# Stores of two sequences split and put off around the first FFT stages of an FFT-mix-FFN kernel

## Chip, cores and metric

The kernel runs on one core of a Trainium2 chip. The metric is the device time of one execution in microseconds (us); lower is better.

## What is computed

The input `x` is 8 sequences of 3008 rows of 256 float32 values. The first part goes through a Fourier transform along the sequence, a complex mixing of the 256 channels with a bias, a soft threshold, and the inverse transform; the second part is a gated FFN over all 24064 rows.

```python
X = np.fft.rfft(x, axis=1)                      # 8 x 1505 x 256, complex
Yr = Xr @ w_r - Xi @ w_i + b_r
Yi = Xr @ w_i + Xi @ w_r + b_i
Yr = np.sign(Yr) * np.maximum(np.abs(Yr) - 0.01, 0.0)      # and Yi likewise
y = np.fft.irfft(Yr + 1j * Yi, n=3008, axis=1).astype(np.float32)
...
gate = 1.0 / (1.0 + np.exp(-(y @ w_gate)))      # 256 -> 1536
out = gate * (y @ w_val) @ w_out                # 1536 -> 256
```

## The kernel before

The transform of length 3008 is split as 47 x 64. A sequence passes through four stages, and between them its data goes through DRAM, since each stage wants it in another layout:

- **Stage A, 47 points** (`load_a`, `fwd_a`, `store_a`). A sequence's 8 blocks `h` of 384 KB are loaded to `xf` tiles; four matmuls with the table `fa_sb` transform each (two for the first half, two for the second); ScalarE and VectorE copy the result back over the same `xf` tile; the tile is stored to the DRAM tile `zd[b]`, 96 rows of it, two for each of the 48 values of `q`.
- **Stage B, 64 points** (`load_b`, `fwd_b`, line 237). A step works on two values of `q`, one from each of two groups; there are NP = 12 steps and two more that drain the pipeline. `load_b(b, q)` loads `zf`, 256 KB, rows `4q` to `4q + 3` of `zd[b]`: what one step reads was written by all 8 stores of stage A. `mf_sb` is the step's table.
- **Mix and inverse of stage B** (`mix4` for the first sequence, line 293; `inv_b`, line 305). The mix of step `q - 1` and the inverse of step `q - 2` (table `mi_sb`) run beside the forward of step `q`; the result `vz` goes to the DRAM tile `vd[b]`.
- **Inverse of stage A** (`load_v`, `inv_a`, line 340). A unit `u` loads `vf`, 192 KB, and makes 188 columns of `y`, split into a high and a low part by ScalarE and VectorE (`split_y`).

The FFN (`ffn1`, lines 399 to 401, and `ffn2`) works on chunks of 512 columns and 12 slices `f` of the hidden dimension. The first chunk needs the units 0, 1 and 2. Its weights come as 64-bit floats (`raw`), and are converted beside the first sequence's steps and the first chunk (`load_part`, `start_part`, `ops`).

The first sequence is done alone, then the second sequence's transform, and later ones, run beside the FFN. The order of this beginning is written out by hand in the `with tc.manual_schedule()` blocks: stage A of sequence 0, then the first four blocks (`EARLY`) of stage A of sequence 1, then the steps `q` of stage B with the remaining four blocks after the last of them, then the three inverse units and the first chunk of the FFN. Nearly all transfers are issued by SyncE, in the order of the code. GpSimd issues those of `vd` in the first sequence, the last four stores of sequence 1, and those of later sequences' half blocks (`azh`, line 199).

At three places TensorE is given matmuls whose result nobody reads (`keep_warm`): WARM = 13 at the start, WARM_Z = 10 between stage A and the first step, and WARM_V = 5 between the first and the second inverse unit (line 836).

The DRAM tile is what a load waits for: a `zf` load waits for the 8 stores to `zd[0]`, and a `vf` load for the 12 stores to `vd[0]`.

Of the kernel before, what the change touches and what calls it, by code (L numbers as in the profile page):

```python
# [9 lines left out]
F32 = mybir.dt.float32  # L10
# [9 lines left out]
R2, R1 = 47, 64  # L20
NK2 = 24
NQ = 2 * NK2
# [5 lines left out]
FFT_BANKS, L1_BANKS, L2_BANKS = 3, 3, 2  # L28
# [4 lines left out]

LAST_GAP, SIDE_GAP = 20, 3
PRE = 2
WARM = 13
WARM_Z, WARM_V = 10, 5
EARLY = 4
AT_FIRST = 3
NCONV = 7  # L40
# [69 lines left out]
def tile_fft_mix_ffn(ctx: ExitStack, tc, x, w_r, w_i, b_r, b_i, w_one, w_out, mf, mi, mis, fa, fb, out):  # L110
# [39 lines left out]
    fa_sb = cw.tile([2 * R2, 2 * NQ], F32, name="fa_sb")  # L150
    nc.scalar.dma_start(fa_sb, fa)

    zd = [tc.dram_tile([NQ, R1, D], F32, name=f"zd{b}") for b in range(B)]
    vd = [tc.dram_tile([NQ, R1, D], F32, name=f"vd{b}") for b in range(B)]
    td = tc.dram_tile([NH, 2, P, 8 * P], F32, name="td")
    md = tc.dram_tile([NK2, P, 2, P], F32, name="md")
    yd = tc.dram_tile([CT, P, B * S - T0], F32, name="yd").rearrange("t p n -> p t n")
    xv = x.rearrange("b u p (h c) -> b u p h c", c=D)
    zv = [z.rearrange("q (j h) c -> (q j) h c", j=2) for z in zd]
    vv = [v.rearrange("q (j h) c -> (q j) h c", j=2) for v in vd]  # L160

    held = {}
# [22 lines left out]

    def store_a(b, h, queue=nc.sync):
        queue.dma_start(zv[b][:, 4 * h:4 * h + 4], held.pop(("x", b, h))[:2 * NQ])

    def load_half(b, h):
        xf = r2k("xfh").bitcast(F32)  # L190
# [35 lines left out]

    def load_b(b, q):
        zf = p2.tile([P, 2, D], F32, tag="ld", bufs=NLD, name="zf")
        nc.sync.dma_start(zf, zd[b][4 * q:4 * q + 4].rearrange("(q a) n c -> (a n) q c", q=2))
        held["z", b, q] = zf  # L230

    def fwd_b(b, q, m, full):
# [251 lines left out]
    def ffn_units():  # L484
        units, todo = [], {}
        seq = [(c, f) for c in range(NPL) for f in range(NF)]

        def own(c):

            return range(-(-c * CW // UT), -(-(c + 1) * CW // UT))  # L490

        for c in range(1, NPL):
            at = (c - 1) * NF
            for i, u in enumerate(own(c)):
                todo.setdefault(at + (0, 3, 6)[i], []).append(lambda u=u: load_v(u))
                todo.setdefault(at + (3, 6, 9)[i], []).append(lambda u=u: inv_a(u))
            todo.setdefault(at + 1, []).append(lambda c=c: carry(c))

        def unit(n):
            c, f = seq[n]  # L500
            if n == 0:
                for i, u in enumerate(own(0)):
                    if i == 1:
                        w = w1h[:, 0].rearrange("p i t n -> p (i t n)")
                        keep_warm(bank("warm", "l1", L1_BANKS), w[:, :P], w, WARM_V)
                    inv_a(u)
            ffn1(c, f)
            for t in todo.pop(n, ()):
                t()
            if n >= LAG and n - LAG < len(seq) - BEHIND:  # L510
                ffn2(*seq[n - LAG])
        return [lambda n=n: unit(n) for n in range(len(seq))], own(0), own(NPL - 1)[-1] + 1
# [346 lines left out]
    with tc.manual_schedule():  # L859
# [2 lines left out]
        load_a(1, 0)  # L862
        for h in range(na):
            fwd_a(0, h)
            store_a(0, h)
            if h in (1, 3, 4):
                load_a(1, {1: 1, 3: 2, 4: 3}[h])
            if h == 2:
                load_mix()
# [4 lines left out]
        load_bias4()  # L874
        load_part()
        mfs[2] = load_mf(2)
        for h in range(EARLY):
            fwd_a(1, h)
            if h == 1:
                wi_sb = mix_weights()  # L880
        keep_warm(bank("warm"), zero[:, :P], zero, WARM_Z)
        for q in range(NP + 2):
            if q + 2 < NP:
                load_b(0, q + 2)
            if 0 <= q - 1 < NP:
                mis_[q - 1] = load_mi(q - 1, True)
            if q < 2:
                for h in range(q * EARLY // 2, (q + 1) * EARLY // 2):
                    store_a(1, h)
            if q == 3:  # L890
                nc.sync.dma_start(fb_sb, fb)
# [33 lines left out]
        for h in range(EARLY + 1, na):  # L925
            ops(left.pop(0), 0)
            fwd_a(1, h)
            store_a(1, h, nc.gpsimd)
        ops(left.pop(0), 0)
    p0s.close()  # L930
    p3 = p3s.enter_context(tc.tile_pool(name="p3", bufs=2, side="right", reuse_waits="tile"))
    with tc.manual_schedule():
        for u in own0:
            load_v(u)
        load_part()
        halves(AT_FIRST)
# [157 lines left out]
```

## Time and profile before

| | us |
|---|---|
| median of 3 runs | 2819.46 (2818.62 to 2820.18) |
| profiled execution | 2820.81 |
| its span, first to last instruction | 2819.0 |
| TensorE busy in it | 2802.4 |
| VectorE busy | 2082.3 |
| ScalarE busy | 1309.6 |
| GpSimd busy | 710.5 |

The span is that of one execution taken by the hardware profiler; the profiled execution's own time is 1.8 us longer, with what lies around the span. PE is TensorE, DVE VectorE, ACT ScalarE, POOL GpSimd, SP SyncE; a `q` behind an engine's name is its queue of issued transfers. L12 is line 12 of the kernel. The granted clock is a share of TensorE's full clock: 1.00 is 2.4 GHz, 0.50 is 1.2 GHz.

### The profile page before, as it was taken

The numbers are of one execution on the slowest core, as the hardware profiler recorded it, in microseconds if no ns is written. First come the engines' busy times: TensorE is split into PE (matmuls) and PEld (weight loads), VectorE is DVE, ScalarE is ACT, GpSimd is POOL, SyncE is SP. The second block draws the span as 40 slices with busy tenths as digits, with TensorE's granted clock in tenths as the row PEclk, the third lists the DMA queues.
The fourth block names the chain that finished last, engine by engine and source line by source line (L and its number), as shares of the span: only waits on it lengthen the run. The fifth ranks groups of instructions, "written<-read, shape, count | busy, mean of one in ns | idle before, by whom it ended". The sixth has DMA issues, their size and how long they took to land.

```text
span 2819.0 us, 38251 instructions
## 1 busy us (share of the span) xinstructions
PE 2802.4 (99%) x13896; PEld 2308.1 (82%) x13896; DVE 2082.3 (74%) x3109; ACT 1309.6 (46%) x2276; POOL 710.5 (25%) x638
## 2 busy tenths in 40 slices
PE   9999999999999999999999999999999999999999
PEld 6678888888899888888888888888888888888887
DVE  5777778667787536777777777777777777777776
ACT  4664544545455444444444444444444444444443
POOL 0211010224100002333333333333333343333321
PEclk9999999999999999999999999999999999999999
DMA  9866544666554661000000000000000000000000
GB/s 296 257 213 194 170 143 149 199 184 192 165 152 140 186 187 38 30 15 16 30 31 27 4 31 31 31 16 15 31 30 16 15 30 31 30 1 30 30 16 15
DMA packets 173469, 241.01 MB, mean 85 GB/s; under 512 B 14592, under 2 KB 124896, under 8 KB 173280
## 3 DMA queue, kind: packets, MB, share of 16 engines
q1 hardware_dynamic: 163776, 214.93, 24.8%
q0 software_dynamic: 9408, 23.60, 2.5%
q8 instruction: 110, 1.80, 0.3%
q14 instruction: 79, 0.65, 0.1%
q10 hardware_dynamic: 96, 0.04, 0.0%
HBM read 134.17 MB, written 104.33 MB: 85 GB/s over the span
## 4 chain that ended last, share of the span: by engine, by line
PE 94%; DVE 2%; DMA 2%; ACT 1%; issue 0%; SPq 0%; DVEq 0%; ACTq 0%
PE pd L659 11%; PE pa L659 11%; PE pc L659 11%; PE po L636 8%; PE po L635 8%; PE po L634 8%; PE pm L271 6%; PE pb L659 5%; PE pia L340 4%; PE pb L237 3%; PE pa L176 2%; PE pg L399 2%; PE pg L401 2%; PE pg L400 2%; PE pv L399 2%; PE pv L400 2%
## 5 line engine op out<-in xcount | busy, mean ns | idle before, releaser
L636 PE MATMUL po<-hl,w 128*128 128x512 f32 x912 | 362.5, 397 | 0.0
L635 PE MATMUL po<-hh,w 128*128 128x512 f32 x912 | 361.5, 396 | 0.0
L634 PE MATMUL po<-hh,w 128*128 128x512 f32 x912 | 360.8, 396 | 0.0
L718 POOL TENSOR_TENSOR c<-c,c 128x512 f32<-128x512 f32 x114 | 147.7, 1296 | 831.0 <-DVE c L714 640.1
L659 PE MATMUL pa<-a,w1h 128*128 128x512 f32 x912 | 284.0, 393 | 0.0
L659 PE MATMUL pc<-s,w1h 128*128 128x512 f32 x912 | 283.7, 392 | 0.0
L714 DVE TENSOR_TENSOR c<-u,pc 128x512 f32<-128x512 f32 x228 | 156.7, 687 | 114.7 <-PE pc L659 106.2
L689 DVE TENSOR_TENSOR u<-u,pb 128x512 f32<-128x512 f32 x228 | 155.3, 681 | 88.8 <-PE pb L659 62.6
L606 ACT CAST hh<-v 128x512 fp32r<-128x512 f32 x114 | 70.7, 620 | 306.2 <-DVE v L699 306.2
L636 PEld LDWEIGHTS po<-hl,w 128*128 128x128 f32 x912 | 171.5, 188 | 41.9
L634 PEld LDWEIGHTS po<-hh,w 128*128 128x128 f32 x912 | 172.0, 189 | 40.9
L635 PEld LDWEIGHTS po<-hh,w 128*128 128x128 f32 x912 | 171.0, 188 | 40.8
L659 PEld LDWEIGHTS pa<-a,w1h 128*128 128x128 f32 x912 | 171.2, 188 | 40.1
L659 PEld LDWEIGHTS pc<-s,w1h 128*128 128x128 f32 x912 | 171.0, 188 | 37.6
L610 POOL TENSOR_TENSOR hl<-c,hh 128x512 fp32r<-128x512 f32 x114 | 152.4, 1337 | 186.1 <-ACT hh L606 186.1
L271 PE MATMUL pm<-w_sb,xsh 128*128 128x256 f32 x1008 | 189.4, 288 | 1.4 <-ACT xf L177 1.1
L659 PE MATMUL pc<-s,w1l 128*128 128x512 f32 x456 | 177.5, 389 | 0.0
L659 PE MATMUL pa<-a,w1l 128*128 128x512 f32 x456 | 177.0, 388 | 0.0
L720 DVE TENSOR_TENSOR u<-u,pd 128x512 f32<-128x512 f32 x228 | 156.9, 688 | 24.5 <-DVE c L714 0.9
L693 DVE TENSOR_TENSOR v<-v,pc 128x512 f32<-128x512 f32 x228 | 156.6, 687 | 24.4 <-DVE v L691 0.5
L691 DVE TENSOR_TENSOR v<-u,pd 128x512 f32<-128x512 f32 x228 | 156.9, 688 | 24.0 <-DVE u L689 0.5
L685 ACT COPY u<-pa 128x512 f32<-128x512 f32 x228 | 133.7, 586 | 78.7 <-PE pa L659 78.6
(174 smaller groups left out, 6738.7 us busy)
## 6 DMA issues: line engine op xcount, KB each, us to landing
zf<-zd SPq DMA_DIRECT2D x96, 256.0 KB, 3.6
vf<-vd SPq DMA_DIRECT2D x128, 192.0 KB, 3.1
out_dram<-ot SPq DMA_DIRECT2D x93, 256.0 KB, 2.2
vd<-vz SPq DMA_DIRECT2D x84, 256.0 KB, 2.9
ypair<-yd SPq DMA_DIRECT2D x19, 1024.0 KB, 5.0
yd<-yf SPq DMA_DIRECT2D x103, 188.0 KB, 3.0
xf<-in_x_dram SPq DMA_DIRECT2D x48, 384.0 KB, 4.1
zd<-xf SPq DMA_DIRECT2D x44, 384.0 KB, 3.4
```

Source lines behind the costliest of these rows:

```text
L271: nc.tensor.matmul(o, l, r, start=(i == 0), stop=(i == len(mms) - 1))
L610: sub_(hl, h, hh)
L634: nc.tensor.matmul(o, wh, hh, start=(f == 0), stop=False)
L635: nc.tensor.matmul(o, wl, hh, start=False, stop=False)
L636: nc.tensor.matmul(o, wh, hl, start=False, stop=(f == NF - 1))
L659: nc.tensor.matmul(o, l, r, start=not more and l is wh and r is xh, stop=l is wl, skip_group_check=more)
L689: add(u, u, b)
L691: add(v, u, d)
L693: add(v, v, c)
L714: add(c12, u, c)
L718: nc.gpsimd.tensor_mul(c12, g12, c12)
L720: add(u, u, d)
```

## The change

The DRAM tile `zd[0]` becomes two: `zd0a` holds the rows of steps 0 to 3 (SOON = 4), `zd0b` those of steps 4 to 11. Each of the 8 stores of sequence 0 becomes two, of 32 rows (128 KB) and of 64 rows (256 KB). The small ones stay where the whole stores were. The large ones stay there for the first three blocks (WHOLE = 3); those of blocks 3, 4 and 5 go behind the loads of the first two steps, of the bias, one weight block and two tables; those of blocks 6 and 7 go behind the third step's load. The four early stores of sequence 1 move from steps 0 and 1 to steps 1 and 2. Its last three stores (blocks 5, 6 and 7) go from GpSimd to SyncE, between the second and the third `vf` load. WARM_Z falls from 10 to 4, and the five warm-up matmuls between the inverse units are gone.

```diff
 PRE = 2
+SOON = 4
+WHOLE = 3
 WARM = 13
-WARM_Z, WARM_V = 10, 5
+WARM_Z = 4
...
-    zd = [tc.dram_tile([NQ, R1, D], F32, name=f"zd{b}") for b in range(B)]
+    zd = [None] + [tc.dram_tile([NQ, R1, D], F32, name=f"zd{b}") for b in range(1, B)]
+    zd0 = [tc.dram_tile([4 * n, R1, D], F32, name=t) for n, t in ((SOON, "zd0a"), (NP - SOON, "zd0b"))]
...
+    def store_a0(h, late):
+        at = slice(8 * SOON, 2 * NQ) if late else slice(0, 8 * SOON)
+        nc.sync.dma_start(zv0[late][:, 4 * h:4 * h + 4], held["x", 0, h][at])
...
-        nc.sync.dma_start(zf, zd[b][4 * q:4 * q + 4].rearrange("(q a) n c -> (a n) q c", q=2))
+        z, at = (zd[b], q) if b else (zd0[q >= SOON], q % SOON if q < SOON else q - SOON)
+        nc.sync.dma_start(zf, z[4 * at:4 * at + 4].rearrange("(q a) n c -> (a n) q c", q=2))
...
             if n == 0:
-                for i, u in enumerate(own(0)):
-                    if i == 1:
-                        w = w1h[:, 0].rearrange("p i t n -> p (i t n)")
-                        keep_warm(bank("warm", "l1", L1_BANKS), w[:, :P], w, WARM_V)
+                for u in own(0):
                     inv_a(u)
...
         for h in range(na):
             fwd_a(0, h)
-            store_a(0, h)
+            store_a0(h, 0)
+            if h < WHOLE:
+                store_a0(h, 1)
...
         mfs[2] = load_mf(2)
+        for h in range(WHOLE, na - 2):
+            store_a0(h, 1)
...
-            if q < 2:
-                for h in range(q * EARLY // 2, (q + 1) * EARLY // 2):
+            if q == 0:
+                for h in range(na - 2, na):
+                    store_a0(h, 1)
+            elif q < 3:
+                for h in range((q - 1) * EARLY // 2, q * EARLY // 2):
                     store_a(1, h)
...
             fwd_a(1, h)
-            store_a(1, h, nc.gpsimd)
...
-        for u in own0:
+        for i, u in enumerate(own0):
+            if i == 2:
+                for h in range(EARLY + 1, na):
+                    store_a(1, h)
             load_v(u)
```

SyncE's transfers from the last `xf` load of sequence 1's early blocks to the third step's load. Before (`zd_77` is sequence 0's DRAM tile):

```order
L171 DMA xf<-in_x_dram 96x1024
L187 DMA zd_77<-xf_133 96x1024
L187 DMA zd_77<-xf_135 96x1024
L187 DMA zd_77<-xf_137 96x1024
L204 DMA mf_sb<-in_mf_dram 128x2x128
L229 DMA zf<-zd_77 128x2x256 x2
L204 DMA mf_sb<-in_mf_dram 128x2x128
L760 DMA bias_98<-in_b_r_dram 64x256
L760 DMA bias_98<-in_b_i_dram 64x256
L807 DMA raw_217<-in_w_one_dram 128x1024
L204 DMA mf_sb<-in_mf_dram 128x2x128
L229 DMA zf<-zd_77 128x2x256
```

The same stretch with the change, and the two stores behind it:

```order
L196 DMA zd0a<-xf_134 32x1024
L196 DMA zd0a<-xf_136 32x1024
L196 DMA zd0a<-xf_138 32x1024
L213 DMA mf_sb<-in_mf_dram 128x2x128
L239 DMA zf<-zd0a 128x2x256 x2
...
L196 DMA zd0b<-xf_130 64x1024
L196 DMA zd0b<-xf_132 64x1024
L196 DMA zd0b<-xf_134 64x1024
L239 DMA zf<-zd0a 128x2x256
L196 DMA zd0b<-xf_136 64x1024
L196 DMA zd0b<-xf_138 64x1024
L213 DMA mf_sb<-in_mf_dram 128x2x128
```

The last three stores ahead of the first two `zf` loads are a third of their size, and three of the large ones now stand between those loads and the third.

SyncE's transfers at the start of the FFN, before (`vd_85` is sequence 0's):

```order
L191 DMA xfh<-in_x_dram 96x512 x4
L323 DMA vf<-vd_85 96x512 x3
L807 DMA raw<-in_w_out_dram 128x1024
L191 DMA xfh<-in_x_dram 96x512 x3
L323 DMA vf<-vd_85 96x512
```

With the change (`zd_77` is now sequence 1's DRAM tile):

```order
L200 DMA xfh<-in_x_dram 96x512 x4
L333 DMA vf<-vd_86 96x512 x2
L192 DMA zd_77<-xf 96x1024 x3
L333 DMA vf<-vd_86 96x512
L814 DMA raw<-in_w_out_dram 128x1024
```

Three stores have come between the second and the third `vf` load. They left GpSimd, whose transfers there were, before:

```order
L187 DMA zd_78<-xf 96x1024
L313 DMA vd_85<-vz 128x2x256
L187 DMA zd_78<-xf 96x1024 x3
L199 DMA zd_79<-azh 96x512 x7
```

Of these, the row of three is gone with the change, and the `azh` stores follow the last `vd` store.

## Rows read from the trace of the kernel before

**Rows 1.** The page: busy times, and the chain of work that ended last.

```profile
PE 2802.4 (99%) x13896; PEld 2308.1 (82%) x13896; DVE 2082.3 (74%) x3109; ACT 1309.6 (46%) x2276; POOL 710.5 (25%) x638
PE 94%; DVE 2%; DMA 2%; ACT 1%; issue 0%; SPq 0%; DVEq 0%; ACTq 0%
```

**Rows 2.** Timeline, TensorE, first steps: start us, us, instructions [idle before <-releaser].

```profile
28.33 2.56 PE L836 MATMUL warm<-zero 128*128 128x512 f32 x10
32.32 1.13 PE L237 MATMUL pb<-mf_sb,zf 128*128 128x128 f32 x8 [1.43 <-issue]
33.84 1.13 PE L237 MATMUL pb<-mf_sb,zf 128*128 128x128 f32 x8 [0.39 <-DMA mf_sb<-in_mf_dram]
...
37.53 0.28 PE L293 MATMUL pm<-wi_sb,xsl 128*128 128x256 f32 x1
39.48 1.13 PE L237 MATMUL pb<-mf_sb,zf 128*128 128x128 f32 x8 [1.68 <-DMA zf<-zd]
```

**Rows 3.** The chain of waits, same stretch: start us, us to landing, transfer.

```profile
3.18 10.38 DMA xf<-in_x_dram
...
13.57 8.18 DMA wf<-in_w_r_dram
...
21.83 7.47 DMA zd<-xf
...
33.16 6.18 DMA zf<-zd
```

**Rows 4.** Timeline, SyncE's queue: start us, us of issuing, transfers.

```profile
29.39 0.89 SPq L229 DMA_DIRECT2D zf<-zd  x2
```

**Rows 5.** Stretches: busy us (instructions) by engine, granted clock, DMA share, GB/s.

```profile
37.80:39.50 1.70, 0.03 (x2) 0.05 (x1) 1.18 (x3) 0.72 (x1) 0.00 (x0) 1.00 1.03 403
40.00:45.00 5.00, 5.00 (x43) 4.89 (x41) 3.66 (x7) 2.69 (x5) 0.00 (x0) 1.00 1.06 387
98.00:104.00 6.00, 5.46 (x21) 2.73 (x19) 2.87 (x5) 3.34 (x7) 2.58 (x5) 1.00 0.91 272
```

**Rows 6.** Timeline, TensorE, inverse units and the first FFN matmul.

```profile
101.18 1.10 PE L340 MATMUL pia<-fb_sb,vf 96*128 96x94 f32 x8
102.06 1.40 PE L836 MATMUL warm<-w1h 128*128 128x512 f32 x5
104.16 1.99 PE L340 MATMUL pia<-fb_sb,vf 96*128 96x94 f32 x16 [0.69 <-DMA vf<-vd]
106.78 0.54 PE L399 MATMUL pg<-yth,w1h 128*128 128x512 f32 x1 [0.62 <-ACT yth L332]
```

**Rows 7.** The chain of waits, start of the FFN.

```profile
94.32 3.54 DMA vd<-vz
...
98.48 5.54 DMA vf<-vd
```

**Rows 8.** DMA issues at 98.12: transfer, count, KB, us to landing.

```profile
vf<-vd SPq DMA_DIRECT2D x1, 192.0 KB, 2.9
```

**Rows 9.** Timeline, GpSimd and VectorE, the last stores of the second sequence.

```profile
96.39 0.62 POOL L187 DMA_DIRECT2D zd<-xf  x1 [1.33 <-issue]
...
100.18 0.51 POOL L187 DMA_DIRECT2D zd<-xf  x1 [1.28 <-ACT w1h L792]
...
98.98 0.68 DVE L177 COPY xf<-pa 96x512 f32<-96x512 f32 x1
```

**Rows 10.** Stretches, start of the FFN, columns as in rows 5.

```profile
108.00:108.50 0.50, 0.50 (x3) 0.40 (x2) 0.18 (x1) 0.48 (x2) 0.00 (x0) 0.50 1.23 402
```

**Rows 11.** Timeline, TensorE: first and last of eight FFN matmuls, then of eleven.

```profile
107.25 0.79 PE L400 MATMUL pg<-ytl,w1h 128*128 128x512 f32 x1
...
110.40 0.44 PE L401 MATMUL pv<-yth,w1l 128*128 128x512 f32 x1
...
113.34 0.39 PE L400 MATMUL pg<-ytl,w1h 128*128 128x512 f32 x1
...
115.66 0.40 PE L401 MATMUL pv<-yth,w1l 128*128 128x512 f32 x1
```

More of the change, by code (lines that the diff above doesn't have):

```diff
@@ L158, in tile_fft_mix_ffn @@
     xv = x.rearrange("b u p (h c) -> b u p h c", c=D)
-    zv = [z.rearrange("q (j h) c -> (q j) h c", j=2) for z in zd]
+    zv = [z and z.rearrange("q (j h) c -> (q j) h c", j=2) for z in zd]
+    zv0 = [z.rearrange("q (j h) c -> (q j) h c", j=2) for z in zd0]
     vv = [v.rearrange("q (j h) c -> (q j) h c", j=2) for v in vd]
```

## Prediction

> **What bounds the kernel now.** I read the page first: TensorE is busy for 99% of the span, and it makes up 94% of the chain that ended last [rows 1]. So a change pays where TensorE still waits on that chain, and only there. I then read TensorE's timeline at the two places that the change touches, and beside each the chain of waits, which says what ended the idle time.
>
> The first place is the start of the 64-point steps. After the ten warm-up matmuls of line 836 TensorE idles 1.43 us, at the second step 0.39 us, and before the third step it idles from 37.81 (the end of the first mix) to 39.48, 1.68 us, for a load of `zf` [rows 2]. The chain says what was late: the last store of the first sequence, issued at 21.83, takes 7.47 us to land; the two first `zf` loads go out behind it at 29.39; and the third `zf`, issued at 33.16, takes 6.18 us [rows 3, 4]. The chain shows a second thing: the load of `wf` goes out at 13.57, when the `xf` load issued eight places earlier has landed (3.18 + 10.38), and the last store goes out at 21.83, when that `wf`, again eight places earlier, has landed (13.57 + 8.18). So SyncE keeps eight transfers under way, and a new one in the list takes a place. While TensorE waits for the third `zf` and behind it, the transfers move 403 and 387 GB/s [rows 5]; the queue is full, not idle.
>
> The second place is the start of the FFN. TensorE does the first inverse unit at 101.18, five warm-up matmuls at 102.06, and waits 0.69 us until 104.16 for the second `vf`; the third unit follows without a gap, and the first FFN matmul comes at 106.78 after 0.62 us for the split [rows 6]. The chain: the last `vd` store lands 3.54 us after 94.32, and the second `vf` takes 5.54 us from 98.48 [rows 7], where the first took 2.9 from 98.12 [rows 8]. Beside it GpSimd stores `zd` at 96.39 and 100.18, with a third store between them [rows 9].
>
> In all, TensorE idles 3.5 us at the first place and 1.3 us at the second. With the clock that is lost after the second (below, 1.5 us) no more than about 6.3 us lies there to be won, and 0.2% of this kernel, about what a measurement can tell from no change, is 5.6 us.
>
> **The change, part by part.** *Split stores, first sequence.* Eight stores of 384 KB become 16, of 128 KB (rows for steps 0 to 3) and 256 KB (the rest). Ahead of the first `zf` load there now stand all eight small ones and three large ones, so 5 x 256 KB = 1.31 MB less. At 387 GB/s [rows 5] that is 3.4 us; the least I would grant is 2.5 us, since there are three more transfers with an issue and a landing of their own, and the last small store is still the eighth behind `wf`. I take 3.0 us. The first step then starts at about 29.3 instead of 32.32. Six warm-up matmuls fewer (line 836; ten took 2.56 us, so 1.5 us) cost and gain nothing: TensorE only waits behind them, and the `zf` sets the start.
>
> *The stores put off.* Three of the large stores (0.79 MB, 2.0 us at 387 to 403 GB/s) now stand ahead of the third `zf` load. Everything else ahead of it (the two bias loads, one `raw`, two `mf`) is as before. So it lands 3.0 - 2.0 = 1.0 us earlier, at 38.3 instead of 39.34. This is the term that decides: whatever the first two steps gain beyond it, TensorE waits for again at the third. Its bounds are 0.5 us (first term 2.5) and 3.0 us (the stores cost the loads behind them nothing). I take 1.0. The last two large stores and the four stores of the second sequence come after this load. What hides them is the slack of the later loads: after the third step TensorE's timeline shows no wait for a `zf` up to the last step. I cost them at nothing. If that cover went, one step would wait for 384 KB, 1 us.
>
> *The longer wait itself.* The first mix now ends about 3.0 us earlier, at 34.8, and the third `zf` is there at 38.3: TensorE idles 3.5 us in one piece where it idled 1.68. After the idle pieces of 1.43 and 1.68 the granted clock stood at 1.00 (2.4 GHz) from 40 to 45 [rows 2, 5], but around 108 it was 0.50 (1.2 GHz), after 1.3 us of idle time with only the short inverse matmuls between [rows 6, 10]. Its price there: eight matmuls from 107.25 to 110.40 are 0.45 us apart, and at the full level ten steps take 113.34 to 115.66, 0.23 us apart [rows 11]; 7 x 0.22 = 1.5 us. A piece of 3.5 us is twice the longest after which the clock held, so I expect one such stretch here. Its cost lies between 0 and 1.5 us; I take 1.2, since part of it may fall into the wait. The Trainium skill speaks against the change here: "TensorE: Matmul & The Clock Gate", section "HAM oscillation — how this bites in real kernels", says that a wait for a transfer between bursts of matmuls throttles the clock, so that the next burst starts cold. By that rule the stretch comes; if the rows at 39.48, where the clock held after a wait, were the whole story, it would not, and the sum would be 1.2 us lower.
>
> *Second sequence's last stores.* Three stores of 384 KB leave GpSimd's queue and go on SyncE's, behind the second `vf` and ahead of the third. That frees the second `vf`: it should land as soon after its issue as the first did, 2.9 us [rows 8], instead of 5.54. But the third unit sets the start of the FFN. Before, its data was there by 105.15, when the second unit's half of the 1.99 us was done [rows 6]. Now its load waits in line behind 1.18 MB: 2.9 us at 403 GB/s, 4.3 us at the 272 GB/s of this stretch [rows 5], after about 101.4, and then takes 0.5 us itself. That is 104.8 to 106.2, so -0.35 to +1.05 us against 105.15. SyncE also stands still until the last copy that it stores is done (98.98 + 0.68 [rows 9]), and so issues the third `vf` some 1 us later than before. Behind the third `vf` wait one `raw` and three `xfh` loads, wanted after 107. I take 0 for this part. The five warm-up matmuls that go from here (1.4 us) lay in the wait and cost nothing; they did not keep the clock up before, and I expect the same stretch at half speed after it as before. The Trainium skill, "DMA: Bandwidth & Descriptors", section "Issuing engines are not separate DMA queues", says that all queues share the same 16 engines. By that rule moving these bytes to SyncE wins nothing by itself; the order in line is all that changes.
>
> *Sum.* -1.0 + 1.2 + 0 = +0.2 us. The profiled execution took 2820.81 (a span of 2819.0 and 1.8 around it) and would take 2821.0; it lies 1.35 above the median of the three runs shown, so the median goes from 2819.46 to **2819.7**. TensorE is the chain from there on, so what is won or lost here stays to the end.
>
> **Rivals.** *The clock holds* at the third step. For: it held after 1.68 us. Against: the piece is twice as long. Then -1.0 + 0 + 0: 2818.5. *The stores put off cost nothing*, because they fill gaps that the slow loads ahead leave: the third `zf` comes 3.0 us earlier, TensorE idles no longer than before, and the clock holds: 2816.5. For: the third `zf` takes 6.18 us, far more than its size. Against: while TensorE waits for it the queue moves 403 GB/s [rows 5]. *The third `vf` is late*: behind the three stores at the low rate, and with the `azh` stores that GpSimd, rid of the `zd` stores, issues sooner, it lands after 105.15, and each us beyond that is one us for the FFN. At 106.2 and with the clock down at the third step it is +0.2 + 1.05: 2820.7; with a second stretch at half speed 2822.2. This is the slower side. *The change does not do what it says*: one DRAM tile less large would not matter if the first load still waited for all stores; the order shows `zf<-zd0a` ahead of five `zd0b` stores, so I give it nothing.
>
> **How the numbers follow.** The forecast 0.50, the clock holds 0.25, stores free 0.08, third `vf` late 0.17. The range 2816.6 to 2822.2 reaches from the free stores to the late `vf` with a second stretch. For faster by over 0.2% all idle time here and the clock stretch would have to go: 0.02. For slower by over 0.2% the clock would have to stay at half over several steps: 0.03. The rest, 0.95, is no change that can be told.
>
> **What would show it.** In the profile after: the first `zf` issued near 26.4; the first step at about 29.3; a wait for `zf` before the third step of 3 us or more, ending near 38.3; a granted clock of 0.50 somewhere in 36 to 43; the second `vf` landed near 101.4 and the third between 104.8 and 106.2; the first FFN matmul within 1 us of 106.8. The prediction is wrong if the third step starts before 37, if the clock stays at 1.00 up to 100, or if the FFN starts over 2 us from where it did.

## The result and the profile after

The changed kernel takes 2828.46 us (median of 6 runs, 2828.15 to 2830.77), the kernel before beside it 2819.45 (6 runs, 2818.29 to 2820.27). The ratio is 1.0033 with a 95% interval of 1.0022 to 1.0043: slower by 9.0 us. The forecast was 2819.7, its range ended at 2822.2, and "slower by over 0.2%" had a chance of 0.03. The prediction was wrong.

The profiled execution of the changed kernel took 2828.5, 7.7 us more than that of before. Its page, with busy times and the chain, reads as [rows 1] did; TensorE is no busier, so the time went into waits.

```profile
PE 2802.7 (99%) x13885; PEld 2309.8 (82%) x13885; DVE 2081.0 (74%) x3109; ACT 1309.4 (46%) x2276; POOL 707.9 (25%) x635
PE 93%; DVE 3%; DMA 2%; ACT 1%; issue 0%; SPq 0%; DVEq 0%; ACTq 0%
```

TensorE's timeline of the first steps, to be held against [rows 2].

```profile
29.52 1.05 PE L247 MATMUL pb<-mf_sb,zf 128*128 128x128 f32 x8
32.91 2.05 PE L247 MATMUL pb<-mf_sb,zf 128*128 128x128 f32 x8 [2.33 <-DMA mf_sb<-in_mf_dram]
...
38.67 1.13 PE L247 MATMUL pb<-mf_sb,zf 128*128 128x128 f32 x8 [0.21 <-DMA zf<-zd0a]
...
58.53 1.10 PE L315 MATMUL pi<-yc,mi_sb 128*128 128x256 f32 x4 [2.06 <-DVE ys L305]
```

The first step starts at 29.52 (forecast 29.3) and the third at 38.67 (forecast 38.3, before 39.48). But the wait did not come in one piece at the third step: 2.33 us of it came at the second, for its table `mf_sb`. And at 56.47 there is a wait that before did not have. The chain of waits of the same stretch (start, us to landing) gives the loads of the second and third step:

```profile
27.22 5.55 DMA mf_sb<-in_mf_dram
...
32.79 5.74 DMA zf<-zd0a
```

The wait that ends at 58.53 is put down to `ys`, but that is not what ended it. The `ys` that was done then began at 57.76 and belongs to a later inverse; before, the same inverse began at 57.23, ahead of the `ys` of 57.48. After, from VectorE's timeline, and then before, from TensorE's and VectorE's:

```profile
57.76 0.68 DVE L305 TENSOR_TENSOR ys<-pm,bias 128x512 f32<-128x512 f32 x1
```

```profile
57.23 1.03 PE L305 MATMUL pi<-yc,mi_sb 128*128 128x256 f32 x4
57.48 0.69 DVE L295 TENSOR_TENSOR ys<-pm,bias 128x512 f32<-128x512 f32 x1
```

What came late is the inverse's table `mi_sb`. SyncE issued its load at 50.33 and it took 8.1 us, so it landed at 58.4; before, it went out at 49.34, took 7.3 and was there by 56.6. The DMA issues at these two places, after and before:

```profile
mi_sb<-in_mi_dram SPq DMA_DIRECT2D x1, 128.0 KB, 8.1
```

```profile
mi_sb<-in_mi_dram SPq DMA_DIRECT2D x1, 128.0 KB, 7.3
```

TensorE's timeline at the start of the FFN, to be held against [rows 6]. The first line is the last group of sequence 1's stage A, twelve matmuls behind the last step; its start serves as a mark below (and is what the expectations call the end of the steps). Before, this group started at 92.91.

```profile
94.29 5.74 PE L181 MATMUL pa<-xf,fa_sb 94*96 94x512 f32 x12 [0.78 <-DVE xf L182]
...
102.44 1.92 PE L350 MATMUL pia<-fb_sb,vf 96*128 96x94 f32 x16
110.79 1.99 PE L350 MATMUL pia<-fb_sb,vf 96*128 96x94 f32 x8 [6.43 <-DMA vf<-vd]
113.40 0.79 PE L409 MATMUL pg<-yth,w1h 128*128 128x512 f32 x1 [0.62 <-ACT yth L342]
...
118.51 1.88 PE L181 MATMUL pa<-xfh,fa_sb 94*96 94x512 f32 x4
```

Here is the loss: the third unit waits 6.43 us for its `vf`. SyncE's timeline (start, us of issuing) and the chain give the load's own history. It was issued at 102.26 behind the three stores, and landed 8.39 us later:

```profile
99.49 0.78 SPq L333 DMA_DIRECT2D vf<-vd  x2
100.38 1.83 SPq L192 DMA_DIRECT2D zd<-xf  x3
102.26 1.95 SPq L333 DMA_DIRECT2D vf<-vd  x1
104.26 1.59 SPq L814 DMA_DIRECT2D raw<-in_w_out_dram  x1
105.95 2.50 SPq L200 DMA_DIRECT2D xfh<-in_x_dram  x3
```

```profile
102.26 8.39 DMA vf<-vd
```

SyncE's timeline before, same place: all three `vf` loads, the weight block and the `xfh` loads were out by 103, since the stores were not in this queue.

```profile
98.12 1.45 SPq L323 DMA_DIRECT2D vf<-vd  x3
99.61 1.04 SPq L807 DMA_DIRECT2D raw<-in_w_out_dram  x1
100.76 1.97 SPq L191 DMA_DIRECT2D xfh<-in_x_dram  x3
```

Five stretches after (columns as in [rows 5]; the last columns are the granted clock, the DMA share and GB/s), and then two of before. The second begins at the mark and is 5.99 us long, and so is the first of before:

```profile
32.90:36.30 3.40, 3.39 (x16) 3.40 (x17) 0.69 (x2) 1.00 (x2) 0.00 (x0) 0.50 1.05 402
...
94.29:100.28 5.99, 5.88 (x13) 2.11 (x14) 4.14 (x7) 3.71 (x8) 1.28 (x2) 1.00 0.34 109
...
100.30:110.70 10.40, 4.06 (x22) 2.59 (x20) 2.52 (x5) 3.25 (x6) 1.59 (x3) 0.87 0.95 287
...
108.00:118.20 10.20, 6.79 (x19) 5.53 (x20) 1.90 (x4) 3.69 (x6) 0.00 (x0) 0.50 0.86 265
...
113.40:118.50 5.10, 5.10 (x12) 3.93 (x13) 1.88 (x4) 3.15 (x4) 0.00 (x0) 0.53 0.90 296
```

```profile
92.91:98.90 5.99, 5.88 (x13) 2.11 (x14) 4.13 (x7) 3.71 (x8) 2.44 (x4) 1.00 0.55 170
...
107.10:110.50 3.40, 3.40 (x9) 2.57 (x9) 1.55 (x4) 2.71 (x4) 0.00 (x0) 0.50 1.06 337
```

In the 6 us behind the mark the transfer engines are less busy than before (109 GB/s against 170, so 0.37 MB less, about one store). The first of the three stores, which GpSimd issued at 96.39 before [rows 9], now stands in SyncE's queue, behind its wait for the last `vd` store. Then all comes at once. From 100.30 to 110.70 the core moves 287 GB/s x 10.4 us = 2.98 MB, and the third `vf` is done only at the end of that. TensorE's clock, at half for 3.4 us around the FFN's start before, is at half for 10.2 us here, part of it inside the wait.

So the 7.7 us of the two profiles: 1.4 up to the mark (94.29 - 92.91; 0.8 won by the third step's start and 2.2 lost behind it), 5.2 between the mark and the FFN's first matmul (19.11 against 13.87), and 1.1 behind it, 0.5 of which is the first twelve FFN matmuls at half clock (113.40 to 118.51, 5.11 us; before 106.78 to 111.38, 4.60), and 0.55 a wait that ends at 177.98.

### The profile page after: what moved, and what is told of

The parts are those of the page before. It is cut to its first block, busy times and chain, and to the rows that moved or that the text cites. A ratio compares the mean times of both kernels' runs of the same rounds, so it can differ in the third digit from the quotient of the medians.

```text
span 2826.7 us, 38229 instructions
## 1 busy us (share of the span) xinstructions
PE 2802.7 (99%) x13885; PEld 2309.8 (82%) x13885; DVE 2081.0 (74%) x3109; ACT 1309.4 (46%) x2276; POOL 707.9 (25%) x635
## 4 chain that ended last, share of the span: by engine, by line
PE 93%; DVE 3%; DMA 2%; ACT 1%; issue 0%; SPq 0%; DVEq 0%; ACTq 0%
PE pd L666 11%; PE pc L666 11%; PE pa L666 11%; PE po L643 8%; PE po L642 8%; PE po L641 8%; PE pm L281 6%; PE pb L666 5%; PE pia L350 4%; PE pb L247 3%; PE pa L181 2%; PE pg L409 2%; PE pg L411 2%; PE pg L410 2%; PE pv L409 2%; PE pv L410 2%
```

## The experiments

Each was run beside the kernel before: 2820.33 (23 runs) for only_second, gpsimd_back, stores_last and warm_v, 2820.03 (33 runs) for only_first, no_shift, only_warm and before_vf, 2819.91 (33 runs) for act_third, late_bias, zf_first and before_order, 2819.79 (15 runs) for one_store, before_again and second_again. The difference that is given first is to that kernel. "Below the changed kernel" compares two medians that were taken beside different runs of the kernel before (medians 2819.45 to 2820.33), so it is uncertain by about 1 us more than the intervals say. Every run of before_vf (highest 2826.76) and of gpsimd_back (2827.93) lies below the changed kernel's lowest, 2828.15, and so do ten of eleven of act_third and seven of nine of stores_last.

### Which part costs the time

**only_second**: the kernel before, with nothing but the three stores moved.

```diff
             fwd_a(1, h)
-            store_a(1, h, nc.gpsimd)
...
-        for u in own0:
+        for i, u in enumerate(own0):
+            if i == 2:
+                for h in range(EARLY + 1, na):
+                    store_a(1, h)
             load_v(u)
```

> The kernel before with that one part of the change alone: the three last stores on SyncE between the second and the third vf load; warm-ups and the first steps as before. Theory 'queue': the third vf lands some 8 us after its issue, the FFN starts 5 us later, and the time is 2824 to 2826 against 2819.5. Rival 'first steps': under 2821.

2827.22 us, ratio 1.0026 (1.0016 to 1.0037): +6.9. In its timeline the third unit again waits for its `vf`, which landed 8.28 us after its issue:

```profile
96.60 5.73 PE L176 MATMUL pa<-xf,fa_sb 94*96 94x512 f32 x12 [0.79 <-DVE xf L177]
...
112.45 1.99 PE L340 MATMUL pia<-fb_sb,vf 96*128 96x94 f32 x8 [4.62 <-DMA vf<-vd]
115.07 0.80 PE L399 MATMUL pg<-yth,w1h 128*128 128x512 f32 x1 [0.62 <-ACT yth L332]
```

From the mark to the FFN it is 18.47 us, as in the changed kernel (19.11). The mark itself is 3.7 us later than before, though the code up to it is the same; before_again and second_again, below, take that up.

**only_first**: the changed kernel with its second part undone (stores on GpSimd, five warm-ups between the units).

```diff
             fwd_a(1, h)
+            store_a(1, h, nc.gpsimd)
...
-            if i == 2:
-                for h in range(EARLY + 1, na):
-                    store_a(1, h)
...
+                    if i == 1:
+                        keep_warm(bank("warm", "l1", L1_BANKS), w[:, :P], w, 5)
                     inv_a(u)
```

> The kernel before with the first sequence's part of the change alone (split stores, put-off stores, the second sequence's early stores one step later, 4 warm-ups ahead of the first step); the last three stores on GpSimd and the five warm-ups between the inverse units as before. The run with the stores back on GpSimd was 5.0 us above before, without those five warm-ups. Theory 'first steps': the part costs 3 to 5 us by itself, through a later bias load and a later table at the fifth step and a clock stretch. Rival 'clock': the five warm-ups make the difference, and this one is within 1.5 us of before.

2822.10 us, ratio 1.0009 (1.0000 to 1.0017): +2.1, at the edge of what can be told. The third step's wait came as forecast, 3.15 us up to 38.27, and the clock held all the same; the FFN starts 12.99 us behind the mark:

```profile
38.27 1.13 PE L247 MATMUL pb<-mf_sb,zf 128*128 128x128 f32 x8 [3.15 <-DMA zf<-zd0a]
...
58.63 1.10 PE L315 MATMUL pi<-yc,mi_sb 128*128 128x256 f32 x4 [2.56 <-DMA mi_sb<-in_mi_dram]
...
107.37 0.50 PE L409 MATMUL pg<-yth,w1h 128*128 128x512 f32 x1 [0.62 <-ACT yth L342]
```

The two parts apart give +6.9 and +2.1, together 9.0; the whole change gave +9.0. The intervals are some 5 us wide, so the close agreement is luck, but the second part is most of the price.

**gpsimd_back**: the changed kernel with the stores back on GpSimd, but without the warm-ups between the units (only_first's first two pieces).

> The changed kernel with the three last stores back on GpSimd's queue, where they were before the change. Theory 'queue': the wait for the third vf goes (under 1.5 us in the stretch between the inverse units), and the time is 2822 to 2824; what is left over the kernel before is the first steps' 1.4 us and some clock. If the engine that issues does not matter, only the order, this is within 1.5 us of the run with the stores last.

2825.31, ratio 1.0016 (1.0007 to 1.0025): 3.2 us below the changed kernel's 2828.46. The long wait for `vf` is gone (1.15 us, at the second unit), and the FFN starts 14.38 us behind the mark.

### Why the third vf is late

**before_vf**: the changed kernel, with the stores of blocks 5 and 6 on SyncE ahead of the first `vf` load (and so ahead of its wait), the third behind the last `vf`. The same transfers in the same queue, but not held back.

```diff
             fwd_a(1, h)
+            if h < na - 1:
+                store_a(1, h)
...
-            if i == 2:
-                for h in range(EARLY + 1, na):
-                    store_a(1, h)
             load_v(u)
+        store_a(1, na - 1)
```

> The changed kernel with two of its three last stores on SyncE ahead of the first vf load, and the third store behind the third vf. Theory 'idle queue': the stores cost what they do since SyncE holds them back for the 3.5 us in which it waits for vd, while little is moved (126 GB/s against 215 before); two of them moved in that time give back 2 to 4 us: 2824 to 2826.5, and FFN's first inputs come without a wait of over 2 us. Rival 'ring': any store on SyncE's ring in this stretch costs the same, wherever it stands; then it is 2826 to 2829 as with the stores last.

2824.16, ratio 1.0017 (1.0008 to 1.0025): 4.3 us below the changed kernel. (The 126 and 215 GB/s of the expectation are taken at the same times of two profiles whose marks lie 1.4 us apart; from the mark on it is 109 against 170.) The waits for `vf` shrink to 1.37 us, now at the first unit, and 0.38 at the third.

```profile
104.56 2.63 PE L350 MATMUL pia<-fb_sb,vf 96*128 96x94 f32 x16 [1.37 <-DMA vf<-vd]
107.58 1.99 PE L350 MATMUL pia<-fb_sb,vf 96*128 96x94 f32 x8 [0.38 <-DMA vf<-vd]
```

**act_third**: the changed kernel, its third `vf` load issued by ScalarE. The stores stay where they are; the load no longer stands behind them in a queue.

```diff
-    def load_v(u):
+    def load_v(u, queue=nc.sync):
...
-        nc.sync.dma_start(vf, vv[b][:, h:h + 2])
+        queue.dma_start(vf, vv[b][:, h:h + 2])
...
-            load_v(u)
+            load_v(u, nc.scalar if i == 2 else nc.sync)
```

> The changed kernel with the third vf load issued by ScalarE, so that it has a queue of its own and stands behind none of the three stores; stores, warm-ups and all bytes as in the change. Theory 'line': the third vf is late because it stands in line behind the stores on SyncE; it then lands within 4 us of its issue, TensorE waits under 2 us between the inverse units, and the time falls by 3 to 5 us to 2823.5 to 2825.5. Rival 'bytes': the stores and the azh stores fill the transfer engines whatever the queue; then it still lands 6 us or more after its issue and the time stays above 2826.5. That all of the seven us come back is not expected, since the xfh loads stay behind the stores.

2824.60, ratio 1.0016 (1.0007 to 1.0025): 3.9 us below. The load went out at 101.71, 0.24 us behind the first of the three stores and ahead of the other two, and landed in 4.8 us instead of 8.39, while the core moved 288 GB/s, no more than the 287 of the changed kernel. The edit thus takes the load out of the line and sends it earlier too (in the changed kernel it went out 1.9 us behind the first store); which of the two counts the run doesn't tell. The wait before the third unit is 1.15 us; another, for `xfh`, comes at 116.40:

```profile
vf<-vd ACTq DMA_DIRECT2D x1, 192.0 KB, 4.8
```

```profile
106.61 1.83 PE L350 MATMUL pia<-fb_sb,vf 96*128 96x94 f32 x8 [1.15 <-DMA vf<-vd]
...
116.40 1.07 PE L181 MATMUL pa<-xfh,fa_sb 94*96 94x512 f32 x2 [1.32 <-DMA xfh<-in_x_dram]
```

**stores_last**: the changed kernel, the three stores behind the third `vf` load.

```diff
-            if i == 2:
-                for h in range(EARLY + 1, na):
-                    store_a(1, h)
             load_v(u)
+        for h in range(EARLY + 1, na):
+            store_a(1, h)
```

> The changed kernel with its three last stores of the second sequence put behind the third vf load instead of ahead of it, still on SyncE. Theory 'queue': the third vf was late because it stood behind those stores, so it lands about 3 us after its issue, the FFN starts about 5 us sooner and the time falls from 2828.5 to 2822 to 2824. Rival 'clock': the loss comes from the warm-up matmuls that are gone; then the FFN's first matmuls still run at half speed for 10 us and the time stays above 2826. Rival 'first steps': most of the loss lies before 60 us; then the time stays above 2826 too, with the third vf early.

2826.13, ratio 1.0022 (1.0012 to 1.0032): only 2.3 us below the changed kernel. No unit waits for `vf` any more and the FFN starts 11.6 us behind the mark, the shortest of all. But the next in line pays: the first chunk's `xfh` load takes 9.95 us, and TensorE waits for that. The wait moved on by one consumer. (The profiled execution took 2828.52, above this kernel's median, and its mark is late, at 97.30.)

```profile
108.90 0.49 PE L409 MATMUL pg<-yth,w1h 128*128 128x512 f32 x1 [0.62 <-ACT yth L342]
...
117.93 1.99 PE L181 MATMUL pa<-xfh,fa_sb 94*96 94x512 f32 x2 [4.87 <-DMA xfh<-in_x_dram]
```

**one_store**: the kernel before, with only the last of the three stores moved to SyncE.

```diff
-            store_a(1, h, nc.gpsimd)
+            if h < na - 1:
+                store_a(1, h, nc.gpsimd)
...
+            if i == 2:
+                store_a(1, na - 1)
             load_v(u)
```

> The kernel before with only the last of the three stores (block 7) moved from GpSimd to SyncE, between the second and the third vf load; blocks 5 and 6 stay on GpSimd. Theory 'line' (the third vf load is late by what stands ahead of it on SyncE, three stores of 384 KB that were held back while SyncE waited for vd): two of them are gone from the line, so it costs a third to a half of the +7 us of the three: +2 to +3.5 us, 2822 to 2823.5, the third vf landing in 4 to 6 us. Rival 'place' (any store there costs the same, because the load waits for one more transfer to start, however small): +5 to +7, 2825 to 2827, with a wait for vf of 4 us or more. Rival 'first steps' (the cost is not here, the first steps run late): the wait for vf is short and the steps end after 95.

2823.90, ratio 1.0013 (1.0004 to 1.0022): +4.1, above the 2 to 3.5 of "line" and below the 5 to 7 of "place"; the interval, 1.1 to 6.2 us, reaches both. Its profiled execution (2821.98) speaks for "line": the third `vf` landed 4.26 us after its issue, and only 0.33 us was waited for it, so it is not any store at that place that costs 4 us or more. That execution lies 1.9 us below the kernel's median, and part of the median's +4.1 it does not show.

```profile
106.12 1.10 PE L340 MATMUL pia<-fb_sb,vf 96*128 96x94 f32 x8 [0.33 <-DMA vf<-vd]
```

**warm_v**: the changed kernel with the five warm-ups between the units put back (only_first's last piece), to see whether the clock is behind the loss.

> The changed kernel with the five warm-up matmuls between the first and the second inverse unit put back, nothing else. Theory 'queue': they run inside the wait, and the time stays within 1 us of 2828.5. Rival 'clock': the stretch at half speed at the start of the FFN gets shorter by 5 us or more and the time falls by 2 us or more.

2828.39, ratio 1.0036 (1.0022 to 1.0051): no change. TensorE waits 5.00 us for the third `vf`, and the clock still falls, at 107.7, inside that wait. The lost warm-ups are not the cause of the loss. Where that wait is short they may still count: gpsimd_back and only_first differ by these five matmuls alone and by 3.2 us, and in only_first's profile the clock was full behind the units, in gpsimd_back's at half for 6.8 us. Their intervals overlap, so this is likely and not shown.

### Are the first steps later, or is it scatter

**before_again**: the kernel before, unedited, profiled a second time.

> The kernel before, profiled a second time. The steps ended at 92.91 in the first profile of it, and at 94.07 to 96.60 in profiles of kernels whose first steps have the same code or nearly. If this is scatter from run to run, the steps end somewhere between 93 and 97 here too, and the time follows: an end at 95 goes with about 2821 to 2823. If the moved stores made the first steps late, it ends within 0.5 us of 92.9 again, at 2820 to 2821.

2820.29, in one execution. The mark is at 94.38, not 92.91, with a smaller wait for the third `zf` and waits for `mi_sb` that the first profile did not show. The FFN starts 13.31 us behind it, and the clock held: its first twelve matmuls take 3.13 us (107.69 to 110.82), where the first profile of the same kernel had 4.60. The time did not follow the mark: 2821 to 2823 was expected for a late one.

```profile
39.34 1.13 PE L237 MATMUL pb<-mf_sb,zf 128*128 128x128 f32 x8 [0.77 <-DMA zf<-zd]
...
94.38 5.76 PE L176 MATMUL pa<-xf,fa_sb 94*96 94x512 f32 x12 [0.78 <-DVE xf L177]
...
107.69 0.50 PE L399 MATMUL pg<-yth,w1h 128*128 128x512 f32 x1 [0.62 <-ACT yth L332]
...
110.82 1.88 PE L176 MATMUL pa<-xfh,fa_sb 94*96 94x512 f32 x4
```

**second_again**: only_second's kernel, profiled a second time.

> The kernel with only the three stores moved, profiled a second time. Scatter: the steps end elsewhere than at 96.60, between 92.9 and 96, and the start of the FFN lies 18 to 19 us behind that end again (13.87 in the kernel before), so that the price of the move is 4 to 5 us whatever the first steps did. If the move makes the first steps late: an end near 96.6 again.

2826.65, in one execution. The mark is at 93.31, not 96.60; the FFN again starts 18.71 us behind it, after a wait of 4.86 us for `vf`. So where the first steps end is scatter, and the price of the move is not.

```profile
93.31 5.75 PE L176 MATMUL pa<-xf,fa_sb 94*96 94x512 f32 x12 [0.79 <-DVE xf L177]
...
109.40 1.99 PE L340 MATMUL pia<-fb_sb,vf 96*128 96x94 f32 x8 [4.86 <-DMA vf<-vd]
112.02 0.79 PE L399 MATMUL pg<-yth,w1h 128*128 128x512 f32 x1 [0.62 <-ACT yth L332]
```

### The first part's waits

**no_shift**: gpsimd_back with the four early stores of sequence 1 back at the first two steps.

```diff
-            elif q < 3:
-                for h in range((q - 1) * EARLY // 2, q * EARLY // 2):
+            if q < 2:
+                for h in range(q * EARLY // 2, (q + 1) * EARLY // 2):
                     store_a(1, h)
```

> The run with the stores back on GpSimd, and in addition the second sequence's four early stores at steps 0 and 1 again, not 1 and 2. If these stores push the bias load and the table of step 2 back (the waits of 2.0 to 2.5 us near 56 to 58), those waits go and the time falls by 1.5 to 2.5 us from 2825.3. If it is the stores of blocks 3 to 7 that do it, the time stays within 1 us.

2823.04, ratio 1.0009 (1.0001 to 1.0018): 2.3 below gpsimd_back, with intervals that overlap. In the profile two waits for `mi_sb` (0.98 and 1.86 us, ending at 43.54 and 50.23) stand in place of the one of 2.33 at 58.60.

**late_bias**: only_first with the bias loaded at step 8 and its subtraction at step 10.

```diff
-                load_bias()
+            if q == 8:
+                load_bias()
...
-            if q == 4:
+            if q == 10:
...
```

> The run with the first sequence's part alone (2822.1), with the two loads of bias_sb at step 8 instead of 3 and the subtraction that waits for them at step 10 instead of 4. Theory 'bias': VectorE's wait for the bias stands in front of the sums that TensorE waits for near 56 to 58 us, and the slow broadcast holds back the table behind it; without it that wait of 2 to 2.5 us goes and the time is 2819.5 to 2821. Rival 'stores': the table of step 3 is late because of the put-off stores; then the wait stays over 1.5 us and the time within 1 us of 2822.1.

2821.23, ratio 1.0004 (0.9995 to 1.0013): 0.9 below only_first, less than can be told. Its profiled execution is the lowest of all profiled ones (2818.36): the wait near 58 is gone, and the mark is at 92.98. The inverse's table now goes out at 49.17, without the two bias loads ahead of it, and takes 5.5 us; in only_first it is 50.55 and 7.9. So it is the second half of the theory that fits, the table held back; the sums behind VectorE's wait for the bias were done at 55.61 in only_first, long before the inverse began at 58.63. The first part can then no longer be told from before.

**zf_first**: only_first with all five put-off stores behind the third `zf` load.

```diff
-        for h in range(WHOLE, na - 2):
-            store_a0(h, 1)
...
-                for h in range(na - 2, na):
+                for h in range(WHOLE, na):
                     store_a0(h, 1)
```

> The first sequence's part alone again, with the three large stores of blocks 3 to 5 behind the third zf load instead of ahead of it. By the term of the prediction (2.0 us for these stores) the third zf lands 1.5 to 2.5 us earlier and the third step's wait falls from 3.2 to 1 us or so. If the total falls too, by 1.5 us or more, the wait was the cost; if it stays within 1 us of 2822.1, the wait only moves on to the steps behind it.

2824.91, ratio 1.0015 (1.0006 to 1.0024): 2.8 above only_first, with intervals that overlap. The third step comes 2.5 us earlier, at 35.73, and the next consumers pay (the wait at 40.54, too, ends with the landing of `mi_sb`, at 40.41):

```profile
35.73 1.13 PE L247 MATMUL pb<-mf_sb,zf 128*128 128x128 f32 x8 [0.84 <-DMA zf<-zd0a]
...
40.54 1.10 PE L315 MATMUL pi<-yc,mi_sb 128*128 128x256 f32 x4 [0.85 <-DVE ys L305]
...
58.99 1.10 PE L315 MATMUL pi<-yc,mi_sb 128*128 128x256 f32 x4 [3.85 <-DMA mi_sb<-in_mi_dram]
```

**only_warm**: the kernel before with WARM_Z = 4 and none between the units.

```diff
-WARM_Z, WARM_V = 10, 5
+WARM_Z = 4
...
-                for i, u in enumerate(own(0)):
-                    if i == 1:
-                        w = w1h[:, 0].rearrange("p i t n -> p (i t n)")
-                        keep_warm(bank("warm", "l1", L1_BANKS), w[:, :P], w, WARM_V)
+                for u in own(0):
```

> The kernel before with the warm-up matmuls alone taken as in the change: 4 instead of 10 ahead of the first step, none between the inverse units; all stores as before. Theory 'queue': the waits there are set by transfers, so the time stays within 1.5 us of before. Rival 'clock': the warm-ups kept the clock up, and one or two more stretches at half speed cost 1.5 to 4 us.

2821.42, ratio 1.0006 (0.9997 to 1.0015): +1.4, not to be told from none. Its profile has the clock at half in both places, from 34.3 to 37.7 and from 106.0 to 112.8.

**before_order**: an attempt at a faster kernel on the old stores: the second table ahead of the first `zf`, the third `zf` ahead of bias and weights, the bias at step 8.

```diff
         mfs[0] = load_mf(0)
+        mfs[1] = load_mf(1)
...
-        mfs[1] = load_mf(1)
+        mfs[2] = load_mf(2)
+        load_b(0, 2)
...
-            if q + 2 < NP:
+            if 0 < q < NP - 2:
...
+            if q == 8:
                 load_bias()
...
-            if q == 4:
+            if q == 10:
```

> The kernel before, no store split or moved: the second step's table is loaded ahead of the first zf loads, the third zf ahead of the first bias and weight block, and the two bias_sb loads at step 8. By the waits of the trace of before (0.39 and 1.68 us ahead of steps 2 and 3) up to 2 us are to be won: 2817.5 to 2819.5 against 2820.0. If the transfers behind come late instead, it is 2820 or more.

2820.96, ratio 1.0001 (0.9993 to 1.0010): the same. The waits for `zf` and the table are gone, and one of 2.67 us that ends at 42.99 stands in their place. The profile puts it down to a weight block's conversion, but the inverse's table, issued at 36.77, landed at 42.86, just ahead of that end. None of the runs found a kernel that beats the one before.

## Why the prediction was wrong

Five columns settle where the time lies (us): the start of the mark and of the first FFN matmul, from TensorE's timelines; what lies between; how long the granted clock is 0.50 around the FFN's start; and the time from the mark to the end of the span.

| kernel | stores of blocks 5 to 7 | mark | FFN | between | clock at half | mark to end |
|---|---|---|---|---|---|---|
| before, twice | GpSimd | 92.91, 94.38 | 106.78, 107.69 | 13.87, 13.31 | 3.4, 0 | 2726.1, 2724.1 |
| only_first | GpSimd | 94.38 | 107.37 | 12.99 | 0 | 2723.8 |
| gpsimd_back | GpSimd | 94.35 | 108.73 | 14.38 | 6.8 | 2726.9 |
| one_store | one on SyncE | 94.55 | 107.84 | 13.29 | 0 | 2725.7 |
| changed kernel | SyncE, ahead of third `vf` | 94.29 | 113.40 | 19.11 | 10.2 | 2732.4 |
| warm_v | the same | 93.83 | 112.69 | 18.86 | 10.2 | 2731.5 |
| only_second, twice | the same | 96.60, 93.31 | 115.07, 112.02 | 18.47, 18.71 | 6.8, 10.2 | 2730.3, 2731.5 |
| act_third | the same, third `vf` on ScalarE | 95.38 | 109.06 | 13.68 | 6.8 | 2728.9 |
| before_vf | two ahead of the first `vf` | 94.87 | 110.19 | 15.32 | 10.2 | 2730.1 |
| stores_last | SyncE, behind the third `vf` | 97.30 | 108.90 | 11.60 | 6.8 | 2729.4 |

With the stores on SyncE ahead of the third `vf` the rest behind the mark takes 2730.3 to 2732.4 us, with them on GpSimd 2723.6 to 2726.9 (the five kernels of that kind that are not in the table, only_warm, late_bias, zf_first, no_shift and before_order, lie within the same bounds). act_third and stores_last start the FFN as early as before and still lie 2.0 and 2.5 us above the highest of these: what they gain there is lost again in part behind that start, in the wait for `xfh` and in a clock at half.

- **The step that failed** is the term of the second sequence's last stores: "Now its load waits in line behind 1.18 MB", with the third `vf` landing at 104.8 to 106.2, and "I take 0 for this part". It landed at 110.65, and the term measured 5.2 us in the profile (4.6 to 5.8 over the profiles of before and of the four with the stores at that place); the move alone cost 6.9 in the median. The sign that the prediction named came: the FFN starts 6.6 us from where it did. The mechanism was that of the rival "the third `vf` is late"; I had bounded its size at 1.05. The rate was right (272 GB/s taken, 287 measured). The bytes were not: I counted 1.18 MB of stores and the load's own 0.2, and 2.98 MB moved until it had landed. The missing 1.6 MB are the first two `vf` loads (0.39 MB; nothing had moved from 99.30 to 100.30), the three `azh` stores from GpSimd (0.59), and 0.6 of what was issued behind it, one `raw` and three `xfh` (1.11 in all, landed at 112.7 and later). So a load at the end of a burst shared the engines with its followers too.
- **What I did not price** was SyncE's standstill until the last `vd` store has landed. I charged only its wait for the last copy, with 1 us of later issue. The standstill kept the first store from the quiet stretch before: its copy was done at 97.22, it went out at 100.38, and the 6 us behind the mark moved 109 GB/s against 170. So it came into the same 10 us as everything else. before_vf, which lets two of the stores go earlier, moves 172 GB/s in that stretch and gave 4.3 us back.
- **Position in the queue, or time of issue, counts beside the bytes.** The Trainium skill, "DMA: Bandwidth & Descriptors", section "Issuing engines are not separate DMA queues", says that starting transfers from several engines saves only the sequencer's time; I leaned on that rule with "moving these bytes to SyncE wins nothing by itself; the order in line is all that changes". act_third differs from it: the same load beside the same stores, from ScalarE, landed in 4.76 us instead of 8.39, at the same 288 GB/s. The rule has room for the earlier issue, ahead of two of the stores; the run doesn't separate that from the queue. The gains of act_third (3.9), before_vf (4.3) and stores_last (2.3) don't add up to one sum, as each passes part of the wait on; how the 5.2 us divide between position, time of issue and bytes stays open.
- **The first sequence's stores, -1.0 at the third `zf`**: the size held (third step at 38.67, 38.15 to 38.60 in only_first, gpsimd_back, late_bias and no_shift; forecast 38.3), but it is within the scatter: other runs of the first part show up to 39.55, the old first steps 38.72 (one_store) to 40.80 (only_second), and in the changed kernel's profile most of the wait came a step earlier, for the table.
- **One stretch at half clock, +1.2**: it came in the changed kernel (32.90 to 36.30, granted 0.50), behind a wait of 2.33 us and not at the third step; in only_first's profile the clock stayed at full level behind a wait of 3.15. So the length of the wait ("twice the longest after which the clock held") did not decide it, though such a stretch between 32 and 46 us is in six of the ten profiles with the split stores. And it was not worth 1.2 in the changed kernel: the second step and its mix took 5.55 us at half clock (32.91 to 38.46; before 3.97, 33.84 to 37.81), but the third `zf` landed only at 38.53, so the wait would have taken that time anyway. The Trainium skill's rule in "TensorE: Matmul & The Clock Gate", section "HAM oscillation — how this bites in real kernels", that a wait for a transfer throttles the next burst, agrees with the row of the changed kernel and not with that of only_first.
- **"What hides them is the slack of the later loads ... I cost them at nothing"**: too bold. only_first's and the changed kernel's profiles show a new wait of 2.06 to 2.56 us near 58, for the inverse's table; zf_first, which puts more stores among these loads, makes it 3.85 and the kernel 2.8 us slower. But before_again waits for `mi_sb` there too (0.70 us), and the first part as a whole costs 2.1 us with an interval that begins at 0.
- **Warm-ups at nothing**: not contradicted by the medians (only_warm +1.4, warm_v 0), but "they did not keep the clock up before" rested on one profile. Of the seven profiles with five warm-ups between the units and no long wait there, five have the clock at 1.00 from 100 to 120 us (before_again, only_first, late_bias, zf_first, one_store) and two at half for 3.4 us (before, before_order); the three without them (gpsimd_back, only_warm, no_shift) all have it at half, for 3.4 to 6.8 us. That they were worth something is likely and not shown.
- The **range** rested on one profile of before. Its two profiles differ by 1.5 us at the mark, and only_second's by 3.3 with the same code, which is more than any term of the sum but the one that failed.

## What to carry to other kernels

Before a store goes to another engine's queue, look what that queue waits for at the place where it will stand, and whether the transfer engines are idle meanwhile: a store held back over a quiet stretch comes back in the burst behind it. For a load at the end of such a burst, count more than the bytes ahead of it: what other engines issue beside it and part of what is issued behind it moved first here (2.98 MB, where 1.38 were counted). And where a queue is full, a change of order only passes the wait to the next consumer; the experiments that removed one wait here (stores_last, zf_first, before_order) each grew another.

## What was not expected of the hardware

- The first two `vf` loads of 192 KB landed in 2.58 and 2.69 us, the third, issued 2.4 us after the second, in 8.39; the weight block behind it took 8.4, and behind the same stores in act_third 12.0.
- In such a burst issuing gets slow as well: the single issue of the third `vf` held SyncE for 1.95 us, where the three of before took 1.45 together.
- The clock's fall was not fixed by the length of the wait before it: it held behind 3.15 us (only_first) and fell behind 2.33 (changed kernel); the same kernel before had it at half behind the inverse units in one profile and full in the other, a difference of 1.5 us over the first twelve FFN matmuls.
- A wait's releaser in the profile can be one that only ended at the same time: the changed kernel's wait up to 58.53 is put down to `ys` (done at 58.44), where the table's landing at 58.4 ended it; zf_first at 40.54 and before_order at 42.99 show the same.
